# A turn of the attention's blocks in another order, and its loads in other shapes

## The chip, the cores and the metric

The kernel runs on one core of a Trainium2 chip. The metric is device time in microseconds (us), the median of several runs. The core has five engines that each work through their own queue in order: PE (TensorE, matrix products), DVE (VectorE), ACT (ScalarE), POOL (GpSimd) and SP (SyncE, which here only issues transfers). PE's weight loads (PEld) overlap its products. Transfers between the main memory and the on-chip memory (128 partitions) are spread over 16 DMA engines.

## The reference

A windowed attention feeds a mixture of experts with two experts for each row, and that feeds one with a single expert for each row. Half of the heads see the last 32 positions, the other half every fourth of the last 128.

```python
def reference(q, k, v, ...):                  # q, k, v: (4, 8, 576, 64)
    scores = q @ k.T / sqrt(64)
    mask_plain = (rel >= 0) & (rel < 32)
    mask_dil = (rel >= 0) & (rel < 128) & (rel % 4 == 0)
    attn = softmax(where(mask, scores, -1e9))
    x = (attn @ v)                            # as (2304, 512)
    x = moe(x)                                # 8 experts, 512 -> 1024 -> 512, top two by noisy logits
    return moe2(x)                            # 8 experts, top one, output gated by a sigmoid
```

## The kernel before

**Attention.** The four batches are worked through one after the other, each in 9 banks of two blocks: a block is 64 query rows against 96 keys, for the four heads of one half ("half" 1 is the dilated heads, half 0 the plain ones). The fifth bank of a batch has one block of either half. There are 36 banks and 39 turns: `SKEW = (1, 1, 1)` makes a pipeline in which turn i does `scores` of bank i, `values` of bank i-2, `finish` of bank i-3 and `transposes` of bank i-1. PE, DVE and ACT take this work in the order in which the code is written: PE through `in_order` (L226), DVE and ACT because the attention stands in a manual schedule.

- `scores` (L868): masks and q k products into a bank `a` of PSUM; DVE takes the row maximum `nmx` (L887, L889); ACT makes four exponentials `pe` with their sums (L894).
- `transposes` (L898): four PE transposes of `pe` into bank `t` or `q`; DVE copies one half into `pT` (L904), ACT the other (L906).
- `values` (L909): products of `pT` and `v` into one of two banks `v`; DVE makes the reciprocal of the sums, `rs` (L916, L918), and scales the result into `xo` (L921). `xo` has three buffers.
- `finish` (L924): SP stores `xo` to the scratch `x1` in main memory (L938, L943), PE transposes it into bank `x`, ACT copies that into `xT`. `logits_part` multiplies `xT` with the gates' weights (bank `v`, DVE copy `lgT`, L691), for half 0 alone.

`go_on` is called some six times in a turn and slips in steps of the routing (on DVE, POOL, ACT and PE) that choose the experts' rows. Since `xo` has three buffers, `xo` of bank i can be written only when the store of bank i-3 has landed.

**Loads.** q and k lie with the 64 dimensions of half 0 on partitions 0 to 63 and those of half 1 on 64 to 127, in two buffers each (`qs`, `ks`). v has the keys on partitions: row block j on partitions 32 to 95 and the 32 keys ahead of it on partitions 0 to 31, in three buffers, one for each batch and half. Before the loop `issue` sends the first batch's loads; in turn i of batch b, `more[bi]` holds the loads for batch b+1. Each transfer takes one of eight semaphores in turn, so that SP issues a transfer only when the eighth before it has landed. From the turn on in which the first `xo` is stored, the loads of a turn are issued behind the stores of that turn. In turns 22, 26 and 30 (`Z_AT`) SP fills a third of the scratch `x2` with zeros, in turn 12 the first weights are loaded.

**Experts.** From turn 35 on, the products of expert 0 (whose rows come from the first two batches) fill PE between the last turns, and PE goes on with the experts of the first mixture, then with those of the second. Weights come in 1 MB pieces `raw`, are split into `whi` (ACT, L208) and `wlo` (DVE or POOL, L209), rows are gathered by POOL (`xg`, L705), transposed by PE and split into `xh` (ACT, L711) and `xl` (DVE, L712).

Of the kernel before, what the change touches and what calls it, by code (L numbers as in the profile page):

```python
# [7 lines left out]
F32 = mybir.dt.float32  # L8
# [53 lines left out]
def attention_moe_moe_kernel(  # L62
# [733 lines left out]
    with ExitStack() as actx:  # L796
# [8 lines left out]
        ks = [ak.tile([P, HH, KP + S], F32, name=f"k{i}") for i in range(2)]  # L805
        vs = [ak.tile([P, NB, HH * D], F32, name=f"v{i}") for i in range(3)]
        for k_ in ks:
            nc.vector.memset(k_[:, :, :KP], 0.0)
        for v_ in vs:
            nc.vector.memset(v_[:KP, 0], 0.0)  # L810
        zero = ak.tile([P, P], F32, name="zero")
        nc.vector.memset(zero, 0.0)

        def load_q(b, half, c0=0, c1=S):
            o = half * D
            return qs[b % 2][o:o + D, :, c0:c1], q[b, o:o + D, :, c0:c1]

        def load_k(b, half, c0=0, c1=S):
            o = half * D
            return ks[b % 2][o:o + D, :, KP + c0:KP + c1], k[b, o:o + D, :, c0:c1]  # L820

# [3 lines left out]
        def load_v(b, half, j0=0, j1=NB):  # L825

            vb = v_of(b, half)
            src = v[b, half].rearrange("(j p) d -> p j d", p=QB)
            f = max(j0, 1)
            return [(vb[KP:KB, j0:j1], src[:, j0:j1]),  # L830
                    (vb[:KP, f:j1], src[QB - KP:, f - 1:j1 - 1])]

# [114 lines left out]
        n_dyn1 = dyn_tiles(2 * N + sum(r for _, r in regs1), N + r1.pad, rows1)  # L947
        ZROWS = -(-(N + P) // (32 * len(Z_AT))) * 32

        def zeros(r0, n):  # L950
            return (x2[r0:r0 + n].rearrange("r d -> (r d)").rearrange("(p c d) -> p c d", p=P, d=P),
                    zero[:, None, :].to_broadcast([P, n * DM // P // P, P]))

# [11 lines left out]
        def busy(n, after=None):  # L965

            with tc.issue_after(after) if after is not None else ExitStack():
                for _ in range(n):
                    nc.tensor.matmul(warm, one.to_broadcast([P, P]), one.to_broadcast([P, 224]), start=True, stop=True)

        busy(WARM)
        issue([load_k(0, 1, 0, KB), load_q(0, 1, 0, P), *load_v(0, 1, 0, 2), load_k(0, 1, KB, S), load_q(0, 1, P, S),
               *load_v(0, 1, 2), load_k(0, 0), load_q(0, 0), *load_v(0, 0)])
        for dst, a, b_ in ((wg1, m1_wg, m1_wn), (wg2, m2_wg, m2_wo)):
# [55 lines left out]
        for i in range(len(all_banks) + to_f):  # L1030
            bi = i % n_bi
            if i < len(all_banks):
                bk = Bank()
                bk.b, bk.bi, bk.blocks = all_banks[i]
                queue.insert(0, bk)
                scores(bk)
                if i < len(WARM_1):
                    busy(WARM_1[i], last_pe[0])
            else:
                queue.insert(0, None)  # L1040
            if len(queue) > to_v and queue[to_v]:
                values(queue[to_v])
# [3 lines left out]
            if len(queue) > to_f:  # L1046
# [8 lines left out]
                if half == 0:  # L1055
                    c0, c1 = (j - 1) * QB, S if bk.bi == n_bi - 1 else (j + 1) * QB
                    ready.append((bk.b, c0, c1 - c0, xT, lgT))
            if len(queue) > to_t and queue[to_t]:
                transposes(queue[to_t])
            if i >= E0_AT and 0 in first_x:  # L1060
                first_products(E0_N)

            if i < len(all_banks):
                if bi == 0:
                    more = [[] for _ in range(n_bi)]
                    b = i // n_bi + 1
                    if b < B:
                        for h in (1, 0):
                            f = 0 if h else 4
                            more[f].append(load_k(b, h))  # L1070
                            more[f + 1].append(load_q(b, h))
                            more[f + 2] += load_v(b, h, 0, 4)
                            more[f + 3] += load_v(b, h, 4)
                if i in Z_AT:
                    z0 = Z_AT.index(i) * ZROWS
                    more[bi].append(zeros(z0, min(ZROWS, N + P - z0)))
                if last_st[0] is None:
# [439 lines left out]
```

## Time and profile before

| | us |
|---|---|
| median of three runs (892.93 to 896.59) | 893.58 |
| the profiled execution | 897.35 |
| its span from the first to the last instruction | 895.1 |
| PE busy in it | 846.1 |
| DVE busy in it | 455.4 |
| ACT busy in it | 381.4 |

The profiled execution is 3.8 us above the median. The page gives for each engine its busy time, for slices of the span the granted clock of TensorE (PEclk, 1.00 is the upper of two levels) and what the DMA engines moved. The trace behind it answers questions: windows (busy time, clock and DMA in chosen stretches), the timeline (instructions of one engine, with the idle time ahead of each in brackets and what ended it), and waits (who waited for whom).

### The profile page before, as it was taken

To read this page: it belongs to the slowest core of one execution; us is meant where nothing else is said; L and a number is where in the kernel's file an instruction comes from. 1 tells how busy PE (TensorE), PEld (TensorE's weight loads), DVE (VectorE), ACT (ScalarE), POOL (GpSimd) and SP (SyncE) were. 2 spreads that over 40 slices of the span, in tenths; PEclk is the share of its full clock that TensorE was granted. 3 is DMA by queue.
4 is the path that set the end of the run, shared out by engine and by line. 5 is a ranking of instruction groups with operands and counts; after the bars stand their busy time and mean duration, and the time that the engine had idled before them with its cause. 6 is when DMAs were issued, how large, how long until landed. Compare 5 with 4: busy or idle time off the path is not lost. (4 is left out here: it accounts for less than half of the span.)

```text
span 895.1 us, 15646 instructions
## 1 busy us (share of the span) xinstructions
PE 846.1 (95%) x5844; PEld 730.6 (82%) x5844; DVE 455.4 (51%) x1291; ACT 381.4 (43%) x991; POOL 239.1 (27%) x289
## 2 busy tenths in 40 slices
PE   8799999979999999999999999798999999999994
PEld 6677777868889899889898989786877989898883
DVE  2347688687426224652441616466454646545450
ACT  2446646441425324352442526323323545545451
POOL 5005243253312323232322422412214111221111
PEclk7789999989999999999999999999999999999997
DMA  8969874444327443554352814425543667454630
GB/s 188 203 177 251 237 215 118 132 116 148 57 47 263 117 124 84 173 163 122 86 192 28 265 24 133 119 58 151 116 153 97 217 223 241 165 186 154 212 116 16
DMA packets 77519, 131.83 MB, mean 147 GB/s; under 512 B 5977, under 2 KB 42153, under 8 KB 76992
## 3 DMA queue, kind: packets, MB, share of 16 engines
q1 hardware_dynamic: 64240, 97.27, 35.0%
q0 software_dynamic: 13200, 33.52, 16.1%
q8 instruction: 47, 0.77, 0.4%
q14 instruction: 32, 0.26, 0.1%
HBM read 106.86 MB, written 24.15 MB: 146 GB/s over the span
## 5 line engine op out<-in xcount | busy, mean ns | idle before, releaser
L209 DVE TENSOR_TENSOR wlo<-raw,whi 128x512 fp32r<-128x512 f32 x256 | 165.0, 701 | 123.4 <-ACT whi L208 123.2
L208 ACT CAST whi<-raw 128x512 fp32r<-128x512 f32 x264 | 144.3, 618 | 38.3 <-DMA raw<-in_moe_w_dram 13.0
L226 PE MATMUL a<-xh,whi 128*128 128x256 f32 (+13 forms) x368 | 113.8, 309 | 3.1 <-ACT xh L711 3.1
L226 PE MATMUL a<-xl,whi 128*128 128x256 f32 (+13 forms) x368 | 112.2, 305 | 2.6 <-DVE xl L712 2.6
L226 PE MATMUL a<-xh,wlo 128*128 128x256 f32 (+13 forms) x368 | 112.1, 305 | 2.0 <-issue 2.0
L226 PE MATMUL v<-xh,whi 128*128 128x256 f32 (+13 forms) x368 | 113.1, 307 | 0.0
L226 PE MATMUL v<-xl,whi 128*128 128x256 f32 (+13 forms) x368 | 111.4, 303 | 0.0
L226 PE MATMUL v<-xh,wlo 128*128 128x256 f32 (+13 forms) x368 | 111.3, 302 | 0.0
L226 PE MATMUL a<-whi,hl 128*128 128x512 f32 (+4 forms) x248 | 97.5, 393 | 0.0
L226 PE MATMUL a<-wlo,hh 128*128 128x512 f32 (+5 forms) x248 | 97.0, 392 | 0.0
L226 PE MATMUL a<-whi,hh 128*128 128x512 f32 (+4 forms) x240 | 95.2, 397 | 0.0
L226 PE MATMUL v<-whi,hl 128*128 128x512 f32 (+1 forms) x240 | 94.1, 392 | 0.0
L226 PE MATMUL v<-wlo,hh 128*128 128x512 f32 (+6 forms) x240 | 93.4, 393 | 0.0
L1114 POOL DMA_INDIRECT x_scratch<-y,sca x30 | 49.1, 1635 | 140.1 <-ACT y L1143 81.5
L226 PE MATMUL v<-whi,hh 128*128 128x512 f32 (+1 forms) x200 | 79.3, 397 | 0.0
L767 DVE SCALAR_TENSOR_TENSOR hl<-v,hh 128x256 fp32r<-128x256 f32 (+13 forms) x92 | 42.6, 463 | 69.3 <-ACT hh L766 69.1
L767 DVE SCALAR_TENSOR_TENSOR hl<-a,hh 128x256 fp32r<-128x256 f32 (+13 forms) x92 | 42.6, 463 | 66.3 <-ACT hh L766 66.1
L226 PEld LDWEIGHTS a<-xh,whi 128*128 128x128 f32 x368 | 70.7, 192 | 4.3 <-ACT xh L711 3.5
L226 PEld LDWEIGHTS a<-xl,whi 128*128 128x128 f32 x368 | 70.9, 193 | 3.5 <-DVE xl L712 2.8
L766 ACT ACTIVATE hh<-a 128x256 fp32r<-128x256 f32 (+13 forms) x92 | 38.4, 417 | 82.5 <-PE a L226 81.4
L766 ACT ACTIVATE hh<-v 128x256 fp32r<-128x256 f32 (+13 forms) x92 | 38.4, 417 | 81.0 <-PE v L226 80.7
L226 PEld LDWEIGHTS a<-xh,wlo 128*128 128x128 f32 x368 | 70.8, 192 | 2.3 <-issue 2.3
(376 smaller groups left out, 1558.2 us busy)
## 6 DMA issues: line engine op xcount, KB each, us to landing
raw<-in_moe_w_dram SPq DMA_DIRECT2D x60, 1024.0 KB
raw<-in_moe_w_dram SPq DMA_DIRECT2D x32, 256.0 KB
k<-in_k_dram SPq DMA_DIRECT2D x7, 576.0 KB
q<-in_q_dram SPq DMA_DIRECT2D x7, 576.0 KB
x_scratch<-zero SPq DMA_DIRECT2D x2, 1664.0 KB
x_nextscratch<-xo SPq DMA_DIRECT2D x20, 128.0 KB
v<-in_v_dram SPq DMA_DIRECT2D x6, 320.0 KB
v<-in_v_dram SPq DMA_DIRECT2D x7, 256.0 KB
```

The costliest lines, as they stand in the source:

```text
L208: nc.scalar.copy(hi_, raw_)
L209: (nc.vector if i % 2 == 0 and all_on is None else eng).tensor_sub(lo_, raw_, hi_.bitcast(F32))
L226: r = op(*args, **kw)
L766: nc.scalar.activation(hh[:, f, :n], ph[:, :n], AF.Relu)
L767: nc.vector.scalar_tensor_tensor(hl[:, f, :n], ph[:, :n], 0.0, hh[:, f, :n].bitcast(F32), op0=ALU.max, op1=ALU.subtract)
L1114: nc.gpsimd.indirect_dma_start(out=dst, out_offset=bass.IndirectOffsetOnAxis(ap=idx, axis=0), in_=y, in_offset=None, compute_op=ALU.add)
```

## The change

1. In a turn, `transposes` of bank i-1 moves from the end (behind `finish`) to right behind `scores`. A turn is now: scores i, transposes i-1, values i-2, logits, finish i-3.
2. For the later batches, k and q are loaded for both halves at once on 128 partitions (in turns 0 and 1 of a batch, instead of 0 and 1 for half 1 and 4 and 5 for half 0). For the first batch the first 128 columns come by half, the rest for both halves in one load.
3. v takes one transfer on 96 partitions instead of one on 64 and one on 32; the first block of a batch, which has no keys ahead of it, has one of its own.
4. The zero fills write rows of 512 elements instead of 128; the tile `zero` grows to 128x512.

```diff
+        def load_q(b, half=None, c0=0, c1=S):
+            p = slice(0, P) if half is None else slice(half * D, (half + 1) * D)
+            return qs[b % 2][p, :, c0:c1], q[b, p, :, c0:c1]
...
+            loads = [(vb[KP:KB, :1], src[:, :1])] if j0 == 0 else []
             f = max(j0, 1)
-            return [(vb[KP:KB, j0:j1], src[:, j0:j1]),
-                    (vb[:KP, f:j1], src[QB - KP:, f - 1:j1 - 1])]
+            at_f = src[:, f:j1]
+            (step, _), *others = [list(x_) for x_ in at_f.ap]
+            return loads + [(vb[:, f:j1], bass.AP(at_f.tensor, at_f.offset - KP * step, [[step, KB], *others]))]
...
-        issue([load_k(0, 1, 0, KB), load_q(0, 1, 0, P), *load_v(0, 1, 0, 2), load_k(0, 1, KB, S), load_q(0, 1, P, S),
-               *load_v(0, 1, 2), load_k(0, 0), load_q(0, 0), *load_v(0, 0)])
+        issue([load_k(0, 1, 0, P), load_q(0, 1, 0, P), *load_v(0, 1, 0, 2), load_k(0, None, P, S), load_q(0, None, P, S),
+               *load_v(0, 1, 2), load_k(0, 0, 0, P), load_q(0, 0, 0, P), *load_v(0, 0)])
...
+            if len(queue) > to_t and queue[to_t]:
+                transposes(queue[to_t])
             if len(queue) > to_v and queue[to_v]:
                 values(queue[to_v])
...
-            if len(queue) > to_t and queue[to_t]:
-                transposes(queue[to_t])
...
+                        more[0].append(load_k(b))
+                        more[1].append(load_q(b))
                         for h in (1, 0):
-                            f = 0 if h else 4
-                            more[f].append(load_k(b, h))
-                            more[f + 1].append(load_q(b, h))
-                            more[f + 2] += load_v(b, h, 0, 4)
-                            more[f + 3] += load_v(b, h, 4)
+                            f = 2 if h else 6
+                            more[f] += load_v(b, h, 0, 4)
+                            more[f + 1] += load_v(b, h, 4)
```

How the instructions stand then: on PE, from the scores of turn 5 to the values of turn 6, before:

```order
L226 MATMUL a_537<-k0_258,q0_256 64x96 x8
L226 MATMUL v_556<-v0_260,pT_533 64x64 x8
L226 MATMUL x_570<-ident_103,xo_519 128x128 x2
L226 MATMUL t_577<-ident_103,pe_501 96x128 x4
L226 LDWEIGHTS identb_106
L226 MATMUL a_586<-masks_108,identb_106 128x384
L226 MATMUL a_586<-k0_258,q0_256 64x96 x8
L226 MATMUL v_605<-v1_261,pT_582 64x64
```

The same place after:

```order
L226 MATMUL a_534<-k0_258,q0_256 64x96 x8
L226 MATMUL t_553<-ident_103,pe_499 96x128 x4
L226 MATMUL v_561<-v0_260,pT_510 64x64 x8
L226 MATMUL x_575<-ident_103,xo_525 128x128 x2
L226 LDWEIGHTS identb_106
L226 MATMUL a_582<-masks_108,identb_106 128x384
L226 MATMUL a_582<-k0_258,q0_256 64x96 x8
L226 MATMUL q_601<-ident_103,pe_547 96x128 x4
L226 MATMUL v_609<-v1_261,pT_558 64x64
```

Before, only the scores stand between the transposes that make `pT_582` and the values that read it; after, values, finish, scores and the next transposes stand between those that make `pT_558` and its values.

On DVE, in turn 5, with what each instruction waits for (DMAHW is the semaphore of a transfer from SP), before:

```order
L887 TENSOR_REDUCE nmx<-a 128x4 [waits PE_49]
L889 TENSOR_SCALAR nmx<-nmx 128x4 [waits DVE_49]
L916 TENSOR_SCALAR rs<-sums 128x4 [waits Activation_49]
L918 RECIPROCAL rs<-rs 128x4 [waits DVE_49]
L921 TENSOR_TENSOR xo<-v,rs 128x256 [waits DMAHW0_49,DVE_49,PE_49]
L904 COPY pT<-t 96x256 [waits PE_49]
```

and after:

```order
L890 TENSOR_REDUCE nmx<-a 128x4 [waits PE_49]
L892 TENSOR_SCALAR nmx<-nmx 128x4 [waits DVE_49]
L907 COPY pT<-t 96x256 [waits PE_49]
L919 TENSOR_SCALAR rs<-sums 128x4 [waits Activation_49]
L921 RECIPROCAL rs<-rs 128x4 [waits DVE_49]
L924 TENSOR_TENSOR xo<-v,rs 128x256 [waits DMAHW7_49,DVE_49,PE_49]
```

The copy of `pT` now stands ahead of `xo`, which waits for a store.

On SP, from the sixth transfer of the program to the first store of `xo`, before:

```order
L959 DMA q_256<-in_q_dram 64x4x448
L959 DMA v_260<-in_v_dram 64x7x256
L959 DMA v_260<-in_v_dram 32x7x256
L959 DMA k_258<-in_k_dram 64x4x576 [waits DMAHW0_49]
L959 DMA q_256<-in_q_dram 64x2304 [waits DMAHW1_49]
L959 DMA v_261<-in_v_dram 64x9x256 [waits DMAHW2_49]
L959 DMA v_261<-in_v_dram 32x8x256 [waits DMAHW3_49]
L959 DMA k_259<-in_k_dram 64x4x576 [waits DMAHW4_49]
L959 DMA q_257<-in_q_dram 64x2304 [waits DMAHW5_49]
L959 DMA v_262<-in_v_dram 64x4x256 [waits DMAHW6_49]
L959 DMA v_262<-in_v_dram 32x3x256 [waits DMAHW7_49]
L943 DMA x_nextscratch<-xo 128x256 [waits DMAHW0_49,DVE_49]
```

and from the fifth on, after:

```order
L967 DMA k_258<-in_k_dram 128x4x448
L967 DMA q_256<-in_q_dram 128x4x448
L967 DMA v_260<-in_v_dram 96x7x256
L967 DMA k_258<-in_k_dram 64x4x128
L967 DMA q_256<-in_q_dram 64x4x128 [waits DMAHW0_49]
L967 DMA v_261<-in_v_dram 64x256 [waits DMAHW1_49]
L967 DMA v_261<-in_v_dram 96x8x256 [waits DMAHW2_49]
L967 DMA k_259<-in_k_dram 128x4x576 [waits DMAHW3_49]
L967 DMA q_257<-in_q_dram 128x2304 [waits DMAHW4_49]
L967 DMA v_262<-in_v_dram 64x256 [waits DMAHW5_49]
L967 DMA v_262<-in_v_dram 96x3x256 [waits DMAHW6_49]
L946 DMA x_nextscratch<-xo 128x256 [waits DMAHW7_49,DVE_49]
```

The loads of k and q became wider and fewer, and the second batch's (`k_259`, `q_257`) carry both halves ahead of the first store.

On ACT, after the last turns, where the rows of expert 1 are made ready (`xh`, three tiles in the banks `t`, `x` and `q`, `val` a step of the routing), before:

```order
L1143 ACTIVATE y<-a,wgta_2063 128x512
L208 CAST whi<-raw 128x2x256 x4
L711 CAST xh_2822<-t 128x4x128
L311 ACTIVATE val<-dm 128x5
L711 CAST xh_2822<-x 128x4x128
L208 CAST whi<-raw 128x2x256 x4
L711 CAST xh_2822<-q 128x4x128
```

and after:

```order
L1151 ACTIVATE y<-a,wgta_2058 128x512
L208 CAST whi<-raw 128x2x256 x4
L711 CAST xh_2808<-t 128x4x128
L711 CAST xh_2808<-x 128x4x128
L208 CAST whi<-raw 128x2x256 x4
L711 CAST xh_2808<-q 128x4x128
L311 ACTIVATE val<-dm 128x5
```

The routing's exponential now stands behind the three `xh`; this comes from the scheduler, not from the text of the change.

## Rows read from the trace of the kernel before

**Rows 1.** The page: PE's busy time, its share of the span, its instructions.

```profile
PE 846.1 (95%) x5844; PEld 730.6 (82%) x5844; DVE 455.4 (51%) x1291; ACT 381.4 (43%) x991; POOL 239.1 (27%) x289
```

**Rows 2.** Windows: length, busy us (x) of PE, PEld, DVE, ACT, POOL; PEclk, DMA share, GB/s.

```profile
0.00:6.50 6.50, 5.67 (x37) 4.66 (x37) 2.46 (x44) 0.00 (x0) 5.15 (x25) 1.00 0.49 113
...
12.00:22.00 10.00, 9.84 (x76) 7.36 (x78) 2.87 (x9) 4.59 (x26) 4.79 (x7) 0.50 1.07 218
...
32.00:36.00 4.00, 0.00 (x0) 0.00 (x0) 0.11 (x1) 0.00 (x0) 0.00 (x0) 0.97 0.75 184
36.00:53.00 17.00, 16.30 (x144) 12.71 (x145) 7.69 (x26) 8.29 (x41) 0.00 (x0) 0.50 0.79 204
...
66.00:82.00 16.00, 14.04 (x214) 10.81 (x214) 14.01 (x34) 10.62 (x54) 14.12 (x16) 1.00 0.93 262
...
96.00:114.00 18.00, 16.19 (x209) 12.83 (x210) 13.43 (x58) 10.94 (x57) 5.86 (x17) 0.82 1.01 283
...
170.00:193.00 23.00, 17.36 (x76) 14.46 (x75) 22.07 (x50) 12.23 (x25) 11.46 (x8) 0.85 0.70 212
...
225.00:250.00 25.00, 25.00 (x172) 21.75 (x171) 9.58 (x20) 10.93 (x24) 6.70 (x6) 1.00 0.36 62
```

**Rows 3.** Timeline of PE, 24 to 62 us: start, us, what; in brackets the idle time before.

```profile
27.96 0.88 PE L226 MATMUL a<-k,q 64*64 64x96 f32 x16
...
30.90 0.88 PE L226 MATMUL a<-k,q 64*64 64x96 f32 x16
36.70 1.15 PE L226 MATMUL v<-v,pT 96*64 96x64 f32 x16 [4.92 <-DVE pT L904]
...
53.64 0.88 PE L226 MATMUL a<-k,q 64*64 64x96 f32 x16
...
57.01 0.88 PE L226 MATMUL a<-k,q 64*64 64x96 f32 x16
...
60.38 0.88 PE L226 MATMUL a<-k,q 64*64 64x96 f32 x16
```

**Rows 4.** Timeline of DVE, 28 to 37 us.

```profile
35.89 0.42 DVE L921 TENSOR_TENSOR xo<-v,rs 128x256 f32<-128x256 f32 x1 [5.96 <-DMA x_nextscratch<-xo]
36.23 0.41 DVE L904 COPY pT<-t 96x256 f32<-96x256 f32 x1
```

**Rows 5.** Timeline of SP's queue: the first store of `xo`.

```profile
21.13 0.36 SPq L943 DMA_DIRECT2D x_nextscratch<-xo  x1
```

**Rows 6.** Windows, for the DMA's rate in the last column.

```profile
23.00:30.00 7.00, 6.67 (x96) 5.18 (x93) 4.35 (x16) 4.46 (x22) 0.00 (x0) 1.00 1.07 149
...
42.00:45.00 3.00, 3.00 (x25) 2.35 (x23) 1.02 (x3) 2.21 (x11) 0.00 (x0) 0.50 0.99 303
...
53.00:55.00 2.00, 2.00 (x39) 1.61 (x36) 0.85 (x2) 0.74 (x2) 0.00 (x0) 1.00 1.13 276
...
173.00:175.00 2.00, 2.00 (x10) 1.47 (x9) 1.91 (x7) 0.00 (x0) 0.00 (x0) 1.00 1.00 414
```

**Rows 7.** Timeline of PE: the scores of turn 1.

```profile
12.16 1.55 PE L226 MATMUL a<-k,q 64*64 64x96 f32 x16 [1.65 <-DMA q<-in_q_dram]
```

**Rows 8.** Waits of PE, 53 to 160 us: us in total, times, the longest.

```profile
PE v L226 <- DVE pT L904: 4.6, 9, 1.3
PE v L226 <- ACT pT L906: 1.2, 4, 0.5
```

**Rows 9.** Timelines of ACT (end of turn 5's exponentials) and of DVE (turn 17).

```profile
30.95 0.21 ACT L894 ACTIVATION_READ_ACCUMULATOR pe<-a,nmx 128x1 f32 x1
...
79.00 1.32 DVE L916 TENSOR_SCALAR rs<-sums 128x4 f32<-128x4 f32 x1
```

**Rows 10.** Timelines of PE and ACT, 174 to 190 us.

```profile
185.13 0.44 PE L226 MATMUL a<-xh,whi 128*128 128x384 f32 x1 [3.07 <-ACT xh L711]
188.15 0.69 PE L226 MATMUL a<-xl,whi 128*128 128x384 f32 x1 [2.58 <-DVE xl L712]
...
181.84 0.21 ACT L311 ACTIVATE val<-dm 128x5 f32<-128x5 f32 x1 [3.37 <-DVE dm L310]
```

More of the change, by code (lines that the diff above doesn't have):

```diff
@@ L805, in attention_moe_moe_kernel @@
         ks = [ak.tile([P, HH, KP + S], F32, name=f"k{i}") for i in range(2)]
-        vs = [ak.tile([P, NB, HH * D], F32, name=f"v{i}") for i in range(3)]
+        vs = [ak.tile([KB, NB, HH * D], F32, name=f"v{i}") for i in range(3)]
         for k_ in ks:
@@ L810, in attention_moe_moe_kernel, with load_k @@
             nc.vector.memset(v_[:KP, 0], 0.0)
-        zero = ak.tile([P, P], F32, name="zero")
+        zero = ak.tile([P, DM], F32, name="zero")
         nc.vector.memset(zero, 0.0)
[L814 to L820, printed above, removed]
+        def load_q(b, half=None, c0=0, c1=S):
+            p = slice(0, P) if half is None else slice(half * D, (half + 1) * D)
+            return qs[b % 2][p, :, c0:c1], q[b, p, :, c0:c1]
+        def load_k(b, half=None, c0=0, c1=S):
+            p = slice(0, P) if half is None else slice(half * D, (half + 1) * D)
+            return ks[b % 2][p, :, KP + c0:KP + c1], k[b, p, :, c0:c1]
         def v_of(b, half):
@@ L947, in attention_moe_moe_kernel @@
         n_dyn1 = dyn_tiles(2 * N + sum(r for _, r in regs1), N + r1.pad, rows1)
-        ZROWS = -(-(N + P) // (32 * len(Z_AT))) * 32
+        ZROWS = -(-(N + P) // (P * len(Z_AT))) * P
         def zeros(r0, n):
-            return (x2[r0:r0 + n].rearrange("r d -> (r d)").rearrange("(p c d) -> p c d", p=P, d=P),
-                    zero[:, None, :].to_broadcast([P, n * DM // P // P, P]))
+            m = n // P * P
+            fills = [(x2[r0:r0 + m].rearrange("(p c) d -> p c d", p=P),
+                      zero[:, None, :].to_broadcast([P, m // P, DM]))]
+            if n > m:
+                fills.append((x2[r0 + m:r0 + n], zero[:n - m]))
+            return fills
         b_tiles = [(b + 1) * S // P for b in range(B)]
@@ L1067, in attention_moe_moe_kernel @@
                     if b < B:
+                        more[0].append(load_k(b))
+                        more[1].append(load_q(b))
                         for h in (1, 0):
-                            f = 0 if h else 4
-                            more[f].append(load_k(b, h))
-                            more[f + 1].append(load_q(b, h))
-                            more[f + 2] += load_v(b, h, 0, 4)
-                            more[f + 3] += load_v(b, h, 4)
+                            f = 2 if h else 6
+                            more[f] += load_v(b, h, 0, 4)
+                            more[f + 1] += load_v(b, h, 4)
                 if i in Z_AT:
                     z0 = Z_AT.index(i) * ZROWS
-                    more[bi].append(zeros(z0, min(ZROWS, N + P - z0)))
+                    more[bi] += zeros(z0, min(ZROWS, N + P - z0))
                 if last_st[0] is None:
```

## The prediction

> **What bounds the kernel now.** The page's busy times come first: PE is busy 95% of the span, and of the others (PEld is PE's own weight load) none over 51% [rows 1]. So a change that adds no work to PE can win only what PE waits, and what it loses at the lower of its two clock levels. The chain of waits that the page follows back from the end stays within the experts, so for the attention I read the windows and then the timelines of PE, DVE and SP. In the windows the reader should look for stretches in which PE's busy time is under their length, and for PEclk under 1.00: PE does nothing from 32 to 36 us, runs at 0.50 (the 1.2 GHz level) from 12 to 22 and from 36 to 53, and loses something around 66 to 82, 96 to 114 and 170 to 193 [rows 2]. After that it is full again: 25.00 of 25.00 us between 225 and 250 [rows 2]. The change moves instructions only up to the first tiles of expert 1; what it saves there reaches the end, since PE has its work queued behind it in the same order.
>
> The largest stall, 4.92 us before the values at 36.70, is booked to `pT` [rows 3]. DVE's timeline shows what is behind it: DVE stood 5.96 us at `xo`, waiting for a store of `xo`, and copied `pT` only after that [rows 4]. The first store was issued at 21.13 [rows 5] and its buffer came free at 35.89, 14.8 us later, because it had to pass through a queue of loads. So in this stretch the bound is the DMA queue, and by way of a three-buffer tile it stops DVE, then PE, and then the clock falls.
>
> **The sum, part by part.** Each term is against the profiled execution, 897.35 us.
>
> (a) The wait of turn 1. The scores at 12.16 waited for q [rows 7]; ahead of them SP had sent 96 + 128 + 128 + 32 + 480 + 448 = 1312 KB (64 x 4 x 96 elements of 4 bytes are 96 KB, and so on). Now it is 128 + 128 + 64 + 96 + 896 + 896 = 2208 KB. What pays for that is the rate: a half of q alone on 64 partitions came in at 276 GB/s, 1 MB weights on 128 partitions at 414 [rows 6]. The two loads that matter grow from 928 to 1792 KB, which at 276 and 414 is 3.4 and 4.4 us (950 and 1835 thousand bytes): 1 us later. If the wide loads came no faster it would be 3.2 us later. What comes before it is nearly the same. PE runs at 0.50 behind this point either way [rows 2], and I take 0, with -1.5 to +3 as bounds.
>
> (b) The stall and the slow clock behind it. Before: from the scores at 30.90 to those at 53.64 are four turns in 22.74 us. At full clock such a turn takes 30.90 - 27.96 = 2.94 us, one with logits 60.38 - 57.01 = 3.37 [rows 3]. Three of the one and one of the other are 12.19, so stall and clock together cost 10.55 us.
> When would the first store land now? Ahead of it are 6624 KB instead of 5472 (both halves of the second batch's k and q instead of one). Lower bound: 5 us for the first 416 KB (3.8 at the 113 GB/s of the first 6.5 us [rows 2], and one to land), 4096 KB on 128 partitions at 414 GB/s 10.1 us, 1856 KB of v at the 303 of a stretch with v and stores [rows 6] 6.3, 256 KB on 64 partitions at 276 0.9, so 22.3 us. With 276 for the wide loads it is 27.4. To both comes what slowed the queue to 149 GB/s in seven us [rows 6], in which POOL's small gate and noise loads ran too: against 218 [rows 2] that is a loss of 2.2 us, and some 2 us to land. I take 29. Upper bound: the mean rate that the store saw before, 5600 KB with its own in 35.89 us or 160 GB/s, for 6752 KB: 43.3 us.
> When is it needed? `pT` no longer stands behind `xo`, so PE can go on to the finish of turn 6 before it stops. That is the scores of turn 6, which end at 31.78 [rows 3], plus transposes and values, about 1 us, less about 1 us because turns without the wait are shorter: 31.5 us. So 29 is in time, and the stall goes; with it goes what preceded the fall of the clock. I take the whole 10.5 us. What is late next is nothing on the DMA's side: by then its queue is empty, the later halves of k and q being already there.
> The rule that bears on this is in the Trainium skill, "SBUF — State Buffer", section "Door 1: The DMA port swizzle": 64 partitions reach only 8 of 16 ports, and at 1 MiB it gives 196 GB/s for them against 328 for 128. Our row has 276 for a half of q, more than the page's figure, and 414 for weights; by the page the 4096 KB would take 12.8 us instead of 10.1 and the store would land 2.7 us later than I take it, still at the need, and the sum would stay what it is.
>
> (c) The other waits for `pT` in the attention: 4.6 us by DVE and 1.2 by ACT, in 13 waits [rows 8]. The cause is the tight place between transposes and values that the order shows: now a whole turn lies between them. Two things take some of it back. The transposes of a bank now come right behind the next scores, and must find the exponentials done: those of turn 5 ended at 30.95 + 0.21 = 31.16, the next scores at 31.78 [rows 3, 9], 0.6 us of slack in a turn without routing; every step of the routing that DVE slips in between eats from it. And in 66 to 82 DVE is itself busy 14.01 of 16.00 us [rows 2], because its small operations stand up to 1.32 us beside POOL's split of weights [rows 9]; there a turn can't get much shorter. I take half, 3 us, with 0 and 6 as bounds; the stretch at half clock in 96 to 114 (0.82 [rows 2]) I leave as it is, though a gain is possible.
>
> (d) Expert 1's first tile. PE stood 3.07 + 2.58 us for `xh` and `xl`, and ACT before it 3.37 us for a step of the routing that it took ahead of `xh` [rows 10]. By the order, ACT now makes the three `xh` first. DVE's part, slowed by POOL, stays, so I take 2 us of the 5.65, with 0 and 5 as bounds.
>
> (e) At nothing: v in one transfer has the same 1 KB pieces and bytes; zero fills with longer rows move the same bytes, and PE doesn't wait for them; SP issues 14 transfers fewer, which it has time for; a larger memset falls in DVE's idle start. Stores in a later batch's first turns queue behind 1152 KB instead of 576: 2.9 us at 414 against 2.1 at 276, and `xo` has three turns of room, over 8 us. Without that room each us would be one on PE.
>
> Sum: 0 + 10.5 + 3 + 2 = 15.5, so 897.35 - 15.5 = 881.9 for such an execution. The median of the runs is 3.8 us below it: 893.58 - 15.5, or **878 us**.
>
> **The rivals.**
> *The stall becomes shorter but stays.* For it speaks that the need (31.5) and the landing (29, uncertain by some us) are close. Two us of idle time would be enough that the clock falls as it did: 96 to 114 lost clock with 1.8 us of idle time [rows 2]. Then (b) gives 3 instead of 10.5: 886 us.
> *The transposes' wait replaces the values'.* If PE stands 0.5 to 1 us in each short turn for the exponentials, the clock falls in the turns that now run at 1.00. Ten of those at half clock cost 10 times what (b) shows for one, (22.74 - 4.92 - 12.19) / 4 = 1.4 us: 14 us, which eats the gain: 892 us. Against it speaks the slack of 0.6 us, and that DVE has `nmx` first in its turn in both orders.
> *The wide loads are no faster, and the store comes later: slower.* It has 1152 KB more ahead of it. At the mean rate of before it lands at 43.3 us, and PE, which needs it at 31.5, stands 11.8 us instead of 4.92; the half clock behind it stays. That is 6.9 us more, and with (c) and (d) at their bound of 0 it gives 900 us. It decides from a landing at 31.5 + 4.92 = 36.4 us on, where (b) gains nothing any more; from 41 us on the loss is over 0.5%. Against it speaks the 414 GB/s row; for it, that in 23 to 30 us the queue went at 149 GB/s although DMA was busy all the time.
>
> **How the numbers follow.** Forecast 0.67 (867 to 884), shorter stall 0.15 (886), new wait 0.08 (892), slower 0.10 (900). The best bounds, 1.5 + 12 + 6 + 5, would give 869 and I go 2 us lower for a clock that holds in 96 to 114; upwards the range takes in the second case and the start's +3: 867 to 891, which leaves out the last two cases and a little of the first. A measurement of this kernel can tell about 0.5%, 4.5 us. Faster by more (under 889.1): the first case and nearly all of the second, 0.81; within it 0.10; slower (over 898) 0.09.
>
> **What would show it.** (a) PE's wait for q in turn 1 ends between 11 and 15 us. (b) No idle stretch of PE around 32 to 36, no row of DVE's `xo` with a wait for a store, PEclk 1.00 from about 22 us on, over 350 GB/s while k and q of the second batch come. (c) PE's waits for `pT` gone, waits of the transposes for `pe` under 3 us in sum; the last turn ends 12 us or more earlier. (d) The 5.65 us down to under 4. Wrong it would be if DVE still waits for a store in turn 5, or PE waits for exponentials in most turns at a lower clock.

## The result

The changed kernel takes 885.78 us (median of 15 executions, 881.54 to 890.26), the kernel before 893.34 us beside it (15 executions): a ratio of 0.9915, 95% interval 0.9891 to 0.9939. It is faster, by 7.6 us. I had forecast 878 us, 15.5 us less, and half of that is missing. Two of the kernels below had executions at a lower clock, more than 1.5% above their fastest (one of six with the loads behind the store, two of six with the loads alone and five buffers), and the figures given for them leave these out. The number of the rival "the stall becomes shorter but stays", 886 us, is the one that was measured.

The profiled execution of after took 886.51 us (span 884.4), 10.8 us less than that of before. PE's busy time hardly changed [rows 1]:

```profile
PE 842.0 (95%) x5844; PEld 722.4 (82%) x5844; DVE 452.7 (51%) x1291; ACT 378.9 (43%) x991; POOL 237.3 (27%) x289
```

Windows of after; columns as in [rows 2]: length, busy time of PE, PEld, DVE, ACT, POOL, then PEclk, DMA share, GB/s.

```profile
6.50:12.00 5.50, 2.28 (x37) 1.74 (x37) 1.13 (x5) 2.15 (x6) 2.87 (x16) 0.99 1.06 361
12.00:22.00 10.00, 10.00 (x114) 7.43 (x110) 4.70 (x15) 5.57 (x32) 4.77 (x7) 0.83 1.12 281
22.00:32.00 10.00, 7.71 (x112) 5.78 (x113) 4.19 (x15) 4.87 (x24) 0.00 (x0) 1.00 0.90 227
32.00:36.00 4.00, 4.00 (x41) 2.72 (x43) 2.72 (x10) 3.87 (x22) 0.00 (x0) 0.55 0.67 165
36.00:53.00 17.00, 17.00 (x178) 12.43 (x179) 7.67 (x26) 7.56 (x39) 0.00 (x0) 0.70 0.68 218
```

Three things are to be seen. The clock is back sooner at the start (0.83 in 12 to 22 us, where it was 0.50). The empty stretch of 32 to 36 us is gone, but PE now lacks 2.29 us in 22 to 32. And behind that the clock falls as before, only for a shorter time: 0.55 in 32 to 36 and 0.70 in 36 to 53 us.

Timeline of PE in after: start, us, what; in brackets the idle time before and what ended it.

```profile
11.39 1.08 PE L226 MATMUL a<-k,q 64*64 64x96 f32 x16 [3.22 <-DMA q<-in_q_dram]
...
24.50 0.88 PE L226 MATMUL a<-k,q 64*64 64x96 f32 x16
...
27.03 0.88 PE L226 MATMUL a<-k,q 64*64 64x96 f32 x16
...
28.41 0.69 PE L226 MATMUL v<-v,pT 96*64 96x64 f32 x16
31.38 0.41 PE L226 MATMUL x<-ident,xo 128*128 128x128 f32 x2 [2.29 <-DVE xo L924]
...
46.43 0.88 PE L226 MATMUL a<-k,q 64*64 64x96 f32 x16
49.93 0.88 PE L226 MATMUL a<-k,q 64*64 64x96 f32 x16
53.44 0.88 PE L226 MATMUL a<-k,q 64*64 64x96 f32 x16
```

The scores at 24.50 are those of turn 5, which started at 27.96 before [rows 3]: 3.46 us sooner; those at 27.03 and 46.43 belong to turns 6 and 10 (30.90 and 53.64 before [rows 3]). PE had finished the values of turn 6 at 28.41 + 0.69 = 29.10 us and then wanted the `xo` that DVE could not write. DVE's timeline shows the same wait as [rows 4], shorter and five us earlier:

```profile
30.81 0.42 DVE L924 TENSOR_TENSOR xo<-v,rs 128x256 f32<-128x256 f32 x1 [4.01 <-DMA x_nextscratch<-xo]
```

At the end of the scores of the last turn after is 9.8 us ahead of before, at the end of the program 10.7.

### The profile page after: what moved, and what is told of

It is laid out like the page before. It is cut to its first block, busy times and chain, and to the rows that moved or that the text cites. A ratio compares the mean times of both kernels' runs of the same rounds, so it can differ in the third digit from the quotient of the medians.

```text
span 884.4 us, 15640 instructions
## 1 busy us (share of the span) xinstructions
PE 842.0 (95%) x5844; PEld 722.4 (82%) x5844; DVE 452.7 (51%) x1291; ACT 378.9 (43%) x991; POOL 237.3 (27%) x289
```

## The experiments

**Order and loads apart.** First each half of the change alone. The order alone, put into the kernel before:

```diff
+            if len(queue) > to_t and queue[to_t]:
+                transposes(queue[to_t])
             if len(queue) > to_v and queue[to_v]:
                 values(queue[to_v])
...
-            if len(queue) > to_t and queue[to_t]:
-                transposes(queue[to_t])
```

> The kernel before with the transposes moved ahead of the values, and nothing else; its loads stay as they were. If the waits for pT and expert 1's first tile are what the order is worth, and the stall at 32 us and the clock are the loads' matter, PE's waits for pT go but the stall of xo's buffer stays at 4 to 5 us (store landing at 36, as before) with the half clock behind it: 2 + 1 us less, 890 us, ratio 0.996 to 0.998. The rival, that the order gives most of the change's gain (pT no longer stands behind xo in DVE's queue, so PE has a turn more before it stops): the stall shrinks by a turn, to about 2 us, and the time is 886 us, ratio 0.992.

Measured: 893.28 us, ratio 0.9993 (0.9972 to 1.0014). The order alone is worth nothing, neither the 3 us of my theory nor the 7 of its rival. In its profiled execution the stall did shrink to 2.00 us, at `xo`, as the rival had it, and no wait of the values for `pT` was left, but the clock fell behind the shorter stall all the same, for 13.7 us instead of 17.1. Then the loads alone (the whole diff of the change but these lines):

> The changed loads with the order of before. If the gain up to 60 us comes from the loads (clock back 6.8 us earlier in turns 2 to 5, first store landing at 31 instead of 36), the scores of turn 5 end near 25.4 instead of 28.8, a stall of 2 to 3 us and the half clock behind it stay, and the waits for pT (6 us) stay too: 893.3 - 7.8 + 0 to 1.5, 886 to 887 us, ratio 0.992 to 0.993. The rival, that loads without the order bring nothing because pT stands behind xo and PE stops a turn earlier: stall 5 us, half clock as long as before, only the start's 3.5 us remain or are lost again: 890 to 893 us, ratio 0.996 to 1.000.

Measured: 887.74 us, ratio 0.9927 (0.9898 to 0.9956). The loads alone give what the whole change gives. In its profiled execution DVE's fourth `xo` came at 30.62 us after a wait of 1.25 for the store, and PE, late from a slow start, did not stand for it. The clock held there and fell later, for 13.7 us from 62 us on, behind waits for `pT`, which this order keeps.

**Is the width the cause, or only the sequence?** The changed kernel with its wide loads cut in two:

```diff
-        issue([..., load_k(0, None, P, S), load_q(0, None, P, S),
+        issue([..., load_k(0, 1, P, S), load_k(0, 0, P, S), load_q(0, 1, P, S), load_q(0, 0, P, S),
...
-                        more[0].append(load_k(b))
-                        more[1].append(load_q(b))
+                        more[0] += [load_k(b, 1), load_k(b, 0)]
+                        more[1] += [load_q(b, 1), load_q(b, 0)]
```

> The changed kernel with every wide load of k and q cut into two loads of 64 partitions each, in the same place, with the same bytes; nothing else. If the width of 128 partitions is what made the loads faster, the rate in 6.5 to 12 us falls from 361 to 220 to 280 GB/s, the wait for q in turn 1 grows from 3.2 to 5 to 7 us, the first store lands 3 to 5 us later than 30.8 and the stall of xo grows from 2.3 to over 5 us: 890 to 893 us, ratio 0.996 to 1.000. The rival: two halves in the queue together use all that one wide load uses; rate 340 to 360 GB/s, stall 2 to 3 us, 886 us, ratio 0.9915.

Measured: 898.82 us, ratio 1.0040 (1.0019 to 1.0062): slower than before. One row each of its windows, of DVE's timeline and of PE's:

```profile
6.50:12.00 5.50, 1.50 (x22) 1.06 (x21) 1.13 (x5) 2.15 (x6) 2.88 (x16) 0.96 1.06 226
```

```profile
39.16 0.42 DVE L924 TENSOR_TENSOR xo<-v,rs 128x256 f32<-128x256 f32 x1 [9.83 <-DMA x_nextscratch<-xo]
```

```profile
39.74 0.66 PE L226 MATMUL x<-ident,xo 128*128 128x128 f32 x2 [8.11 <-DVE xo L924]
```

226 GB/s against 361, the store 8.35 us later, the stall 8.11 us instead of 2.29. It is worse than I expected (a stall of over 5 us, 890 to 893 us), and it comes near my third rival, priced at 900 us. Of the 8.35 us, 3.2 are due to the store being issued later (21.93 instead of 18.76 us); from issue to landing it took 17.2 us instead of 12.1. The halves are also twice as many transfers, but in 6.5 to 12 us the DMA engines were as busy as in after (share 1.06 in both rows) and moved less. The width is what pays for loading both halves ahead of the store. The page that the prediction cites, the Trainium skill's "SBUF — State Buffer", section "Door 1: The DMA port swizzle", has 196 against 328 GB/s; the ratio, 0.60, is about that of these two stretches (226 / 361 = 0.63), though our figures are higher.

**Take the link away: more buffers for `xo`.** In the changed kernel, and in the same way in the kernel before:

```diff
         at = actx.enter_context(tc.tile_pool(name="at", bufs=3))
+        at_xo = actx.enter_context(tc.tile_pool(name="at_xo", bufs=5))
...
-            bk.xo = at.tile([P, HH, D], F32, name="xo")
+            bk.xo = at_xo.tile([P, HH, D], F32, name="xo")
```

> The changed kernel with xo in five buffers instead of three, so that DVE need not wait for the first store to land (30.8 us, two turns later is time enough). My theory: the 2.29 us at the transposes of xo start the fall of the clock; without them PEclk stays at 1.00 from 16 to 60 us, and the 6.2 us that are left of the term for stall and slow clock (10.5 - 4.3) go: 885.8 - 6 = 880 us, ratio 0.985. The rival: the clock falls anyway, from what PE did in the turns before; then only the wait itself goes, 2.3 us: 883.5 us, ratio 0.989, with PEclk at 0.70 or less in 36 to 53 us.

Measured: 883.38 us, ratio 0.9895 (0.9864 to 0.9925). In its profiled execution (span 878.6, 5.8 us less than after's) the theory holds:

```profile
22.00:32.00 10.00, 10.00 (x139) 7.54 (x138) 5.79 (x20) 7.75 (x40) 0.00 (x0) 1.00 0.90 235
32.00:36.00 4.00, 4.00 (x65) 2.86 (x64) 3.04 (x12) 3.21 (x18) 0.00 (x0) 1.00 0.51 141
36.00:53.00 17.00, 17.00 (x213) 12.38 (x211) 8.80 (x31) 9.35 (x46) 0.00 (x0) 1.00 0.97 297
```

No stall, and the clock stays at 1.00: the wait of 2.29 us is what the fall of the clock follows on. But the profiled execution is the fastest of its six; the median is only 2.4 us under that of after where I expected 6, and the intervals overlap.

> The kernel before with xo in five buffers instead of three. If the stall of 4.92 us comes from xo's buffer alone and the half clock behind it from the stall, both go: 10.5 us less, 883 us, ratio 0.988, and PEclk is 1.00 from 22 to 60 us. If the clock falls for another reason, only the 4.9 us go: 888.4 us, ratio 0.9945. If five buffers only move the stall to turn 7 (the store of turn 3 landed at 35.9, and turn 7's xo would be wanted at about 37): 893, ratio 1.000.

Measured: 883.53 us, ratio 0.9889 (0.9853 to 0.9925). One tile with two more buffers, and nothing of the change, does about as much as the change. That these 9.7 us are the 10.5 that I had put on stall and slow clock is not shown: in its profiled execution the four turns from turn 6 to turn 10 took 16.16 us instead of 22.74, since the sixth `xo` waited 2.81 us for a store, PE 1.77 us for `pT` behind it, and the clock fell for 6.8 us; 5.2 us came from the start, where the clock happened to hold.

**Move the loads behind the store.**

```diff
-                        more[0].append(load_k(b))
-                        more[1].append(load_q(b))
+                        o = 4 if b == 1 else 0
+                        more[o].append(load_k(b))
+                        more[o + 1].append(load_q(b))
```

> The changed kernel with the second batch's k and q loads issued in turns 4 and 5, behind the first store, instead of 0 and 1. If the first store lands late (30.8 us) because of the 2304 KB of loads queued ahead of it, it lands 4 to 6 us earlier, DVE never waits for xo's buffer, and the time is that of the changed kernel without the stall as five buffers gave it: 883 us, ratio 0.989 (up to 6 us less in the profiled execution). The rival: the store's own way through the queue is slow whatever stands ahead; it lands near 30 us, the stall of about 2 us stays, 886 us, ratio 0.9915.

Measured: 884.05 us, ratio 0.9868 (0.9832 to 0.9905). In its profiled execution the first store was issued at 21.31 us and no `xo` waited for one, the fourth of them at 29.80; in after it took from 18.76 to 30.8. So what stands ahead of the store decides how long it takes. But here too the ratio is only a little under that of after (0.9915), and the intervals overlap.

**Why so little?** A run of the changed kernel with another edit, far behind the attention ("Expert 1's first tile" below), happened to show it. Up to the experts the two kernels are the same, but in this execution q came 0.35 us later and the clock stayed low until 21 us:

```profile
12.00:22.00 10.00, 10.00 (x89) 7.75 (x87) 3.58 (x9) 4.10 (x22) 4.78 (x7) 0.54 1.12 274
...
32.00:36.00 4.00, 4.00 (x66) 2.92 (x62) 2.56 (x10) 3.64 (x20) 0.00 (x0) 1.00 0.61 160
36.00:53.00 17.00, 17.00 (x221) 12.27 (x219) 9.82 (x34) 10.79 (x53) 0.00 (x0) 1.00 0.86 286
...
350.00:400.00 50.00, 47.66 (x261) 41.37 (x261) 25.79 (x72) 18.18 (x37) 13.74 (x18) 0.90 0.50 157
```

```profile
30.14 0.88 PE L226 MATMUL a<-k,q 64*64 64x96 f32 x16
...
41.23 0.88 PE L226 MATMUL a<-k,q 64*64 64x96 f32 x16
```

```profile
30.72 0.42 DVE L924 TENSOR_TENSOR xo<-v,rs 128x256 f32<-128x256 f32 x1 [0.81 <-DMA x_nextscratch<-xo]
```

The store landed at the same time (30.72 against 30.81), but PE came three us later, did not wait, and kept its clock. The scores of turn 10 started at 41.23 instead of 46.43 us, those of the last turn at 133.02 instead of 135.47. So a bad start hides the stall, and here that was worth more than the start: the four turns from turn 6 on took 11.09 us, against 19.40 in after and 22.74 before. That the span is no shorter in the end (884.2 us against 884.4) comes from what follows. The clock fell for 10.2 us from 96 us on, where after kept it, and the edit cost another fall of 10.2 us from 352 us on (0.90 in 350 to 400 us, 1.00 in after). So an execution of these first turns can have no stall that more buffers could take away; how many do, two profiled executions don't show. To test whether a better start brings the stall back, I filled the wait of turn 1 with more of the kernel's filling products (`busy`), with three buffers and, before that, with five:

```diff
-WARM_1 = (4, 8, 8)
+WARM_1 = (36, 8, 8)
```

> The changed kernel with the 36 filling products between the scores of turns 0 and 1, and xo in three buffers as it is. If the landing of the first store (near 30.8 us) is what bounds the first turns, a better clock at the start only brings PE sooner to the wait for xo: the stall grows from 2.3 to 3 to 5 us where the clock held, the half clock of 13.7 us follows it, and the time stays at 885 to 887 us, ratio 0.990 to 0.992, against 0.982 with five buffers. The rival: start and stall are independent; then the start gives its 3 to 4 us here as well: 881 to 882 us, ratio 0.987.

> The changed kernel with five xo buffers and 36 instead of 4 filling products between the scores of turns 0 and 1 (0.11 us each, 3.4 us more), so that PE works while it waits for q (3.2 to 4.7 us in the profiled executions). If the idle time of that wait is what lets the clock fall for 3.4 to 10.2 us from 11 us on, PEclk stays at 1.00 from 6 to 60 us and up to 5 us go: 879 to 881 us, ratio 0.984 to 0.987, and executions differ less. The rival: the filling products delay turn 1 by as much as they save, or the clock falls all the same: 883 us, ratio 0.989 or a little more.

Measured: 887.59 us, ratio 0.9922 (0.9896 to 0.9947) with three buffers, and 878.98 us, ratio 0.9821 (0.9792 to 0.9851) with five. PE with three buffers:

```profile
30.89 0.66 PE L226 MATMUL x<-ident,xo 128*128 128x128 f32 x2 [3.30 <-DVE xo L924]
```

Its windows:

```profile
6.50:12.00 5.50, 5.39 (x69) 4.85 (x69) 1.13 (x5) 2.13 (x6) 2.90 (x16) 1.00 1.06 365
12.00:22.00 10.00, 10.00 (x130) 7.77 (x127) 5.28 (x17) 6.01 (x32) 4.78 (x7) 1.00 1.11 286
22.00:32.00 10.00, 6.70 (x99) 4.81 (x99) 4.07 (x16) 4.83 (x25) 0.00 (x0) 0.85 0.89 230
32.00:36.00 4.00, 4.00 (x39) 3.05 (x37) 2.27 (x8) 3.33 (x18) 0.00 (x0) 0.50 0.56 158
36.00:53.00 17.00, 17.00 (x179) 12.29 (x177) 7.67 (x26) 7.65 (x39) 0.00 (x0) 0.70 0.66 217
```

The start is perfect (1.00 until 29 us), the scores of turn 5 end at 23.88 instead of 25.38, and all of it is lost again in a stall of 3.30 us and 17.1 us of half clock. With three buffers the landing of the first store, at 30 to 31 us, bounds the first turns, whatever a better start gives. By the medians either edit alone gives the changed kernel nothing, or little; both together take it 15.6 us under before (894.54 beside it). That this is the number that I had forecast for the change is chance. Where the pair wins is not shown either: in the profiled execution with five buffers the clock still fell, from 14.4 to 21.2 us, 1.84 us of the wait were left, and the scores of turn 10 came at 40.94 us, later than with five buffers alone (39.35).

**The order without the stall.** The new order costs PE something that I had not counted. Turns without any wait, logits included, are 3.37 us long before (60.38 - 57.01 [rows 3]) and 3.51 after (53.44 - 49.93 above). PEld's timeline (the weight loads) shows where, first before, then after:

```profile
57.82 0.55 PEld L226 LDWEIGHTS v<-v,pT 96*64 96x64 f32 x16
58.43 0.77 PEld L226 LDWEIGHTS v<-xT,wg 128*16 128x16 f32 x8
59.41 0.20 PEld L226 LDWEIGHTS x<-ident,xo 128*128 128x128 f32 x2 [0.21 <-issue]
...
60.38 0.69 PEld L226 LDWEIGHTS a<-k,q 64*64 64x64 f32 x16 [0.26 <-issue]
```

```profile
51.31 0.55 PEld L226 LDWEIGHTS v<-v,pT 96*64 96x64 f32 x16 [0.18 <-issue]
51.93 0.77 PEld L226 LDWEIGHTS v<-xT,wg 128*16 128x16 f32 x8
52.90 0.20 PEld L226 LDWEIGHTS x<-ident,xo 128*128 128x128 f32 x2 [0.21 <-issue]
...
53.43 0.69 PEld L226 LDWEIGHTS a<-k,q 64*64 64x64 f32 x16 [0.26 <-issue]
```

Where weights of 64 columns or fewer follow weights of 96 or 128, the load stands 0.18 to 0.26 us in these rows. Before, that happens once in a turn, at the scores; after, also at the values, which now follow the transposes. With the five buffers I put the transposes one place later (scores, values, transposes, logits, output):

```diff
-            if len(queue) > to_t and queue[to_t]:
-                transposes(queue[to_t])
             if len(queue) > to_v and queue[to_v]:
                 values(queue[to_v])
+            if len(queue) > to_t and queue[to_t]:
+                transposes(queue[to_t])
```

> The changed kernel with five xo buffers, and the transposes one place later: scores, values, transposes, logits, output. My new theory: the place of the transposes costs PE 0.13 us in every turn (a turn with logits is 3.37 us before, 3.50 us with the change, without any wait), since behind the scores they put one more step from products on 64 or 96 rows to products on 128 and back between them (last transpose to the first values 0.20 us, inside such a group 0.11). Then turns go back to 3.37 and 2.39 us and 34 of them give 4.4 us against the changed kernel with five buffers (883.4): 879 us, ratio 0.984, and the waits for pT stay away. The rival: the longer turn belongs to something else (the loads, the buffers), turns stay at 3.50: 883 us, ratio 0.989.

Measured: 886.63 us, ratio 0.9887 (0.9850 to 0.9925), no different from 0.9895 for the changed order with five buffers. The edit did only half of what I expected. Turns without logits went back from 2.53 to 2.39 to 2.45 us; those with logits stayed at 3.50, since there the transposes now stand ahead of the logits' 16 columns. Nor did the waits for `pT` stay away: one of 3.40 us stood at 96.08 us, ahead of a fall of the clock of 6.8 us. PEld's timeline of this kernel, first a turn without logits and then one with them:

```profile
30.57 0.39 PEld L226 LDWEIGHTS q<-ident,pe 128*96 128x96 f32 x4
30.94 0.25 PEld L226 LDWEIGHTS x<-ident,xo 128*128 128x128 f32 x2
...
44.85 0.39 PEld L226 LDWEIGHTS t<-ident,pe 128*96 128x96 f32 x4
45.42 0.77 PEld L226 LDWEIGHTS v<-xT,wg 128*16 128x16 f32 x8 [0.18 <-issue]
```

The order of before, with the new loads and five buffers, and the same with the filling products:

> The changed loads, the order of before, five xo buffers: against the changed kernel with five buffers this undoes the order alone, with no stall of xo in either. If the order gives on one side what it takes on the other (waits for pT of 6 us gone, but 34 turns longer by 0.13 us each, 4.4 us, and DVE later by its fuller queue), the two are within 2 us: 882 to 885 us, ratio 0.988 to 0.991. The rival, that the order is worth the 3 us of my prediction or more once the stall is gone: 886 to 888 us, ratio 0.993.

> The changed loads with the order of before, five xo buffers and the 36 filling products. If order and clock at the start are independent, it differs from the same kernel in the new order by less than 2 us, and is 3 to 5 us under the one without the filling products: 879 to 882 us, ratio 0.984 to 0.988. The rival: the order of before, with its waits for pT of 5 to 6 us, now counts for more since nothing else holds PE up: 884 us, ratio 0.990.

Measured: 881.58 us, ratio 0.9852 (0.9816 to 0.9888), and 878.44 us, ratio 0.9836 (0.9795 to 0.9877). Against 0.9895 and 0.9821 in the new order the difference has one sign in the first pair and the other in the second: the order is worth nothing that can be measured here, with the stall or without it.

**What the loads are worth then.** The kernel before with five buffers and filling products:

> The kernel before with five xo buffers and the 36 filling products; loads and order as before. If with the stall and the start out of the way the narrow loads still bound the first turns (its fifth xo waited for a store until 32.9 us with five buffers), the wide loads are worth 3 to 5 us beside them: 882 to 884 us, ratio 0.987, against 0.9836 with wide loads. The rival: buffers and filling products are all there is to win: 878 to 880 us, ratio 0.983.

Measured: 880.93 us, ratio 0.9880 (0.9831 to 0.9929); with the wide loads it was 0.9836. The intervals overlap, so this stays open. The profiled executions speak for the loads (span 879.3 against 872.6 us, the second the fastest of its six; with the narrow ones PE waited 2.8 us for k at the start, with the wide ones for no load).

**Expert 1's first tile.** The changed kernel with one argument changed:

```diff
-                    nxt["w1"] = load_w(wr1, w1_of(segs[si + 1][0][0]), F, nc.gpsimd if si == 0 else nc.vector)
+                    nxt["w1"] = load_w(wr1, w1_of(segs[si + 1][0][0]), F, nc.vector)
```

> The changed kernel with the low parts of expert 1's first weights all made on DVE instead of some on POOL. If DVE is late with xl for expert 1's first tile because its small routing steps stand beside POOL's subtractions (3.07 us for one on DVE at 168 us), PE's wait of 5.3 us at a<-xl falls to 1 to 3 us: 3 us less, 883 us, ratio 0.988. The rival: DVE gets these subtractions on top (0.69 us each) and is as late as before or later; the wait stays at 5 to 8 us: 886 to 889 us, ratio 0.992 to 0.995.

Measured: 885.32 us, ratio 0.9884 (0.9837 to 0.9930), which can't be told from the changed kernel. PE's waits in its trace, 160 to 365 us (us in total, times, longest):

```profile
PE r L226 <- DVE ohs L391: 2.3, 1, 2.3
...
PE t L226 <- DMA xg<-x_nextscratch,gatf: 1.7, 1, 1.7
PE a L226 <- DVE xl L712: 1.4, 1, 1.4
```

The wait for `xl` did fall, from 5.3 to 1.4 us, so the cause is the right one; but a wait of 2.3 us for another step of DVE (`ohs`, 0.9 in after), with the fall of the clock at 352 us right behind it, and one of 1.7 for a gather took its place.

All runs in one table. The last column is an estimate of mine from the results: the median over a kernel's executions of span times (1 - mean granted clock), which is what PE would lose to the lower level if it was busy all the time.

| kernel | us | ratio | lost to the clock, us |
|---|---|---|---|
| before | 893.3 to 895.2 | 1 | 27.6 to 29.5 |
| changed | 885.78 | 0.9915 | 21.2 |
| order alone | 893.28 | 0.9993 | 27.6 |
| loads alone | 887.74 | 0.9927 | 22.6 |
| changed, loads in halves | 898.82 | 1.0040 | 31.4 |
| changed, loads behind the store | 884.05 | 0.9868 | 19.4 |
| before, five buffers | 883.53 | 0.9889 | 19.4 |
| changed, five buffers | 883.38 | 0.9895 | 21.2 |
| the same, transposes second | 886.63 | 0.9887 | 25.2 |
| loads alone, five buffers | 881.58 | 0.9852 | 16.7 |
| changed, expert 1's weights on DVE | 885.32 | 0.9884 | 22.6 |
| changed, filling products | 887.59 | 0.9922 | 23.9 |
| changed, five buffers, filling products | 878.98 | 0.9821 | 16.6 |
| loads alone, five buffers, filling products | 878.44 | 0.9836 | 13.2 |
| before, five buffers, filling products | 880.93 | 0.9880 | 16.7 |

From before (27.6 where its median was 893.26) to the changed kernel the column falls by 6.4 us, and the median by 7.6: by this estimate the gain is mostly clock.

## Why the prediction was half right

**(a) The start, forecast 0: -3.5 us in the profiled pair.** The wait for q itself was longer (3.22 against 1.65 us) and the scores of turn 1 still ended 1.2 us sooner, all within my bounds. I had written that what comes before this wait is nearly the same; but the first block's k now comes in one load of 128 columns, and a wait of before in turn 0 is gone:

```profile
8.98 0.87 PE L226 MATMUL a<-k,q 64*64 64x96 f32 x14 [1.99 <-DMA k<-in_k_dram]
```

What I had left out is the clock behind it. I wrote that PE runs at 0.50 behind this point either way; in after that lasted 3.4 us instead of 10.2. That this is the change's doing is not shown. With the wide loads and no more filling products the scores of turn 5 started between 24.50 and 27.61 us in seven profiled executions, and the clock was low for 3.4 to 10.2 us; with the loads of before they started at 27.96, 26.98 and 22.80 us in three, and the clock was low for 10.2, 10.2 and 0 us. The wide loads did what I priced (361 GB/s in 6.5 to 12 us).

**(b) Stall and slow clock, forecast -10.5: -3.3 us.** This is the step that failed. Measured as the forecast did it, the four turns from the scores of turn 6 on took 46.43 - 27.03 = 19.40 us instead of 22.74. The mechanism was right: the queue, the three buffers, DVE, PE, the clock. Both sizes were off. The store landed at 30.8 us, not 29, within my bounds. The need was the graver error: I took it from the timeline of before, 31.5 us, though any gain in (a) moves it, and it came at 29.1. A margin of 2.5 us became a lack of 1.7, and as the clock falls behind a wait of 2.29 us just as behind one of 4.92, there was little between all and almost nothing. The one run with 3.30 us shows the same. In the run with expert 1's edit the start was as slow as I had assumed, the need came behind the landing, and the four turns took 11.09 us: there the term came whole, 11.7 us. (It is more than 10.5 because the turn of 2.94 us that I took for one without a wait holds one of 0.33 us for `pT`; without any wait such a turn took 2.39 us in the order of before.) So the term hung on how the start fell out, and a stall that stays was far more likely than the 0.15 that I gave it: I had written myself that need and landing were uncertain by some us.

**(c) The waits for `pT`, forecast -3: -2.6 us in the profiled pair, nothing by the runs of the order alone.** That is from the scores of turn 10 to those of the last turn (89.04 us instead of 91.61); in the run with expert 1's edit they took 91.79. The 5.8 us of waits [rows 8] are gone; no wait for `pT` is left among PE's waits up to 160 us in after, whose largest are

```profile
PE a L226 <- DMA q<-in_q_dram: 3.2, 1, 3.2
PE x L226 <- DVE xo L924: 2.3, 1, 2.3
PE v L226 <- DVE xo L924: 1.9, 2, 1.1
PE q L226 <- ACT pe L897: 1.3, 1, 1.3
```

I took half of them because of DVE and the exponentials. The exponentials cost 1.3 us, once, near 100 us, where in before PE waited as long for `pT` (the longest wait of [rows 8], at 106.41 us). Behind that wait the clock had fallen (0.82 in 96 to 114 us [rows 2]), and behind the wait for the exponentials it fell in the run with expert 1's edit (0.72), but not in after:

```profile
96.00:114.00 18.00, 15.61 (x211) 11.16 (x210) 15.10 (x72) 9.52 (x50) 7.42 (x19) 1.00 0.53 182
```

So some 3 us of the -2.6 (18 x 0.18, an estimate) are a clock that happened to hold, which I had rightly not counted on, and the waits for their part gave nothing. What took their gain back I had at nothing, without saying so. DVE's `xo` now holds PE up for 1.9 us instead of 0.9 in 53 to 160 us, DVE's `xl` for 1.0, and PE's own work is longer in another order: some 34 turns by 0.13 us are 4.4 us, an estimate from the two turn lengths. The Trainium skill's "TensorEngine Tiling (Array Packing)", section "Key Properties", says that a change of the tiling mode drains TensorE; it gives no price, and no run here shows whether these changes of shape are changes of its mode.

**(d) Expert 1's first tile, forecast -2: -0.3 us by its waits.** They were 5.65 us [rows 10] and are 5.31. ACT is early now, as the order had said; but DVE's `xl`, the second row of [rows 10], was the last wait all along. Timeline of DVE, then of POOL and of PE:

```profile
168.25 3.07 DVE L252 TENSOR_TENSOR eq<-eq,erev 128x40 f32<-128x40 f32 x1
...
175.55 0.20 DVE L252 TENSOR_TENSOR eq<-eq,erev 128x40 f32<-128x40 f32 x1
...
177.92 0.68 DVE L712 TENSOR_TENSOR xl<-q,xh 128x512 fp32r<-128x512 f32 x1
```

```profile
168.12 3.13 POOL L209 TENSOR_TENSOR wlo<-raw,whi 128x512 fp32r<-128x512 f32 x2
```

```profile
178.66 0.69 PE L226 MATMUL a<-xl,whi 128*128 128x384 f32 x1 [5.31 <-DVE xl L712]
```

The step that takes 0.20 us at 175.55 took 3.07 at 168.25, beside POOL's subtractions. I had written that this part stays; then I should have taken 0.

**(e)** Nothing was found for the zero fills and v (SP issues 13 transfers of q, k and v fewer, 35 instead of 48, not 14). The sentence of (b) that what is late next is nothing on the DMA's side was wrong: the store itself was late.

**From one execution to the median.** The sum was read in an execution 3.8 us above the median and then taken whole from the median. The profiled executions are 10.8 us apart, the medians 7.6. In the profiled execution of before the mean granted clock was 0.966, by the estimate of the table 30.4 us lost; in 19 other executions of before (median 893.26 us) the median is 27.6. A usual execution had less to win back than the one that I had read.

**The rivals.** The shorter stall came true in the profiled execution, with 3.3 us for a price of 3; that its 886 us was met as well is in part luck, since it had the start at 0 and took its sum whole from the median too. The transposes' wait for exponentials did not: 1.3 us. The third, that the loads come no faster, is close to what the halves showed when the width is taken away: 898.8 us for a price of 900.

**The signs that I had named.** Met were the end of the wait for q (11.39 us), the waits for `pT` gone and under 3 us for `pe`. Not met were the rows of (b) (`xo` waited for a store, PEclk fell), the last turn (9.8 us earlier and not 12) and the 5.65 us of (d), which stayed above 4. Over 350 GB/s came in 6.5 to 12 us, when the first batch's wide loads came; for the second batch's k and q, issued at 8.84 and 11.53 us, the windows can't tell it: 12 to 22 us had 281.

## What to carry to other kernels

When a term hangs on two times, a landing and a need, work both out for the changed kernel: what the same change gains ahead of the wait brings the need forward. If a stall depends on how fast PE comes to it, either edit alone can measure as little, and the pair has to be run (here two more buffers for one tile, and filling products: 0.982). A sum read in one execution holds for that execution: compare its clock with that of the others before taking it from their median. A step that is moved on PE has a price of its own even if no wait changes: look at the weight loads on both sides of its new place.

## What the runs showed of the hardware

In the rows above weight loads stood 0.18 to 0.26 us where weights of 64 columns or fewer followed weights of 96 or 128, and 0.21 us where 128 columns followed 16; from scores to transposes and from values to transposes most rows show no gap.

The lower clock lasted for much longer than the wait ahead of it, and did not grow in step with it: 17.1 us behind 4.92, 13.7 behind 2.29, 17.1 behind 3.30, 20.5 behind 8.11, 6.8 behind 1.77 us. Waits of one length differed too: behind 4.0 us for q it lasted 10.2 us with the loads alone, and behind 4.07 us 3.4 us in the changed kernel with five buffers.

The same bytes in loads of half the width came at 226 instead of 361 GB/s, and the store behind them took 17.2 instead of 12.1 us from issue to landing.
